# New pacing constants for a hand-planned two-layer transformer kernel

## The chip, the cores and the metric

The kernel runs on one core of a Trainium2 chip. The metric is the device time of one execution in microseconds. The engines are TensorE (PE, with its weight loads PEld), VectorE (DVE), ScalarE (ACT), GpSimd (POOL) and SyncE (SP), which here only issues transfers.

## What is computed

Two rounds of the same attention layer and the same feed-forward layer, with the same weights in both rounds, over 2048 tokens of 448 features in bfloat16. Attention has 16 heads of 28 features.

```python
x = A_x
x = x + _A_ref(_layernorm(x), A_wqkv, A_wo)
x = x + _B_ref(_layernorm(x), B_w1, B_b1, B_w2, B_b2)
x = x + _A_ref(_layernorm(x), A_wqkv, A_wo)
x = x + _B_ref(_layernorm(x), B_w1, B_b1, B_w2, B_b2)

# _A_ref: q, k, v of x @ wqkv; p = softmax(q k^T * 28 ** -0.5); (p v) @ wo
# _B_ref: h = relu(x @ w1 + b1); (h * h) @ w2 + b2
```

## The kernel before, in words

**Tiling.** A tile of scores, a unit, is 128 keys x 512: two key blocks of 128 by 256 queries of one head (four key blocks by 128 queries in the last two query blocks). There are 2048 units. They are taken in passes: a pass is one layer, one block of queries, one set g of four heads, and a range of key blocks. The second layer's first passes cover only the first ten key blocks, then the other six, so that they can begin while the first layer's last rows are still in work.

**Groups.** `s_stream` (L1015 on) takes three units at a time. It multiplies them on TensorE into three banks of one PSUM tile `sc` (L1074), and `e_stream` has ScalarE take the exponential of the whole tile in one activation (L1100). There are 683 groups. At each group `apart` may decide that the third unit goes aside: ScalarE then takes two banks, 1024 columns, and VectorE takes the third with GpSimd's help. That way is `a_unit` and `a_rest`: VectorE reads the scores once into integers (L1161), GpSimd or VectorE makes a mantissa line (L1190) and a power of two (L1204), VectorE squares (L1207), either adds one (L1210) or leaves that term to TensorE as a second multiplication with the values, and multiplies the two (L1213).

**Values and chains.** `p_stream` multiplies the exponentials with the values (L1297) and hands the sums on to be normalised. When a block's four sets of heads are done, `chain` does the output projection, the layernorm, the feed-forward layer, and for the first layer the next layernorm and the keys, values and queries of the second layer. All dense matmuls of the chains go through one helper (L782); K, Q and V are written to SBUF at L805, L801 and L833, the layernorm's transposes are at L685 and L697, and the residual sums at L1433.

**What sets the order.** A planner, `Planner.run`, simulates the engines in Python while the program is being written. Each stream offers its next operation; the one that can start earliest goes next, and ties go to the lower rank. Its result is a fixed order of instructions on each engine; nothing of it is decided on the chip. Constants steer it, and `s_stream` replaces some of them at certain groups:

```python
globals().update(PACE.get(gi, {}))
```

The ones that matter here, as `apart` and others use them:

- `FORCE` and `SKIP` are lists of group numbers. A group on the first always sends its third unit aside if buffers, data and position allow it; one on the second never does.
- Otherwise a unit goes aside only if VectorE's planned load over the last `SPAN` us is not above `BUSY` (or `LOW`), and its planned backlog in us not above `TB` (or `TB2`). `LOW` and `TB2` count when the layer's chains are behind a due line that `L1N` and `MARGIN` set. `LEAD` is the number of groups before VectorE's first unit. With fewer than `STOP` = 80 units left, none goes aside.

```python
if len(gbuf) - 1 in FORCE:
    return j
if len(gbuf) - 1 in SKIP or pl.load(SPAN, "DVE") > (LOW if behind(i) else BUSY):
    return None
if max(0.0, pl.clock["DVE"] - now) + left[0] > (TB2 if behind(i) else TB):
    return None
```

- `SPARE` and `VSPARE`: more free buffers than this, and the unit's "add one" becomes a second multiplication on TensorE in place of L1210 on VectorE.
- `MORE` limits how often a group's score matmuls are repeated into the same banks where TensorE would otherwise be idle (L1074 again; the result is the same).
- `C_PRIO`, `V_PRIO`, `V_LATE`, `V_LAST`, `V_AGE`, `V_PAST`, `V_WAIT`, `EPRIO`, `EV`: ranks of VectorE's and GpSimd's operations for the scores, and of the evacuations of the chains' matmuls. `PRE` moves a chain up before its rows are done.
- `KEEP`, `CHUNK`, `NEAR`, `FAR`, `LAG`: how long the multiplications with the values wait, how many of them go together, and how far ahead VectorE's unit is taken.
- `PWAIT`, `PNEAR`, `PORTP`: how VectorE and GpSimd take turns, in the plan, for operations marked as using a shared port.

Of the kernel before, what the change touches and what calls it, by code (L numbers as in the profile page):

```python
# [33 lines left out]
PWAIT = 3.0  # L34
PNEAR = 0.2
PORTP = 0.0
PGAP = 0.08
EPRIO = 6
SPARE = 1
VSPARE = 2  # L40
ASIDE = 2.0
# [6 lines left out]
PRE = 0.5  # L48
# [10 lines left out]
L1N = 5.6  # L59
MARGIN = 1.5  # L60
LOW = 0.85
# [12 lines left out]
SLACK = 0.5  # L74
WINDOW = 2.8
HTURNS = 3
C_PRIO = 1.6
V_PRIO = 8.5
V_LATE = 3.5
V_LAST = 2.5  # L80
V_AGE = 6
V_PAST = 2
# [3 lines left out]
V_WAIT = 5  # L86
NEAR = 3
FAR = 9
KEEP = 6
# [6 lines left out]
LAG = 12  # L96
LEAD = 15
LAST = 690
BUSY = 0.97
TB = 2.2  # L100
TB2 = 0.9
SPAN = 15
# [4 lines left out]
MORE = 1  # L107
# [6 lines left out]
SOON = 0.3  # L114
# [6 lines left out]
CHUNK = 2  # L121
EV = 2.9
# [13 lines left out]
MMC = 0.46  # L136
VGAP = 0.03
QP = 8
FORCE = (21, 50, 64, 78, 99, 101, 106, 137, 153, 155, 160, 179, 215, 218, 222, 233, 252, 300, 305, 324, 334, 363,
         373, 404, 443, 466, 487, 495, 533, 565, 568, 591, 593, 628, 633, 646)  # L140
SKIP = (0, 10, 29, 41, 43, 54, 57, 59, 62, 100, 105, 108, 110, 177, 195, 217, 219, 236, 293, 303, 335, 360, 378,
        383, 389, 395, 400, 408, 411, 418, 442, 467, 470, 471, 481, 494, 504, 544, 549, 558, 563, 571, 584, 588,
        601, 607, 613, 615, 630, 636)
PACE = {
    0: {'BUSY': 1.05, 'LOW': 1.0, 'CHUNK': 2, 'EV': 2.9, 'FAR': 9, 'KEEP': 2, 'L1N': 5.2, 'LAG': 8, 'LEAD': 10,
         'MARGIN': -1, 'MORE': 1, 'PRE': 0.5, 'SLACK': 0.7, 'SPAN': 11, 'TB': 2.0, 'TB2': 0.9, 'V_AGE': 6, 'V_LAST':
         3, 'V_PAST': 2, 'C_PRIO': 1.6, 'V_PRIO': 2.6, 'V_LATE': 6, 'V_WAIT': 5, 'EPRIO': 6, 'ASIDE': 2.0, 'SPARE':
         0, 'VSPARE': 2, 'NEAR': 3, 'SOON': 0.3, 'VGAP': 0.03, 'PWAIT': 3.0, 'PNEAR': 0.2, 'PORTP': 0.0},
    8: {'TB': 2.8, 'SPAN': 8},
    16: {'SPARE': 3, 'V_AGE': 3, 'C_PRIO': 1.2},  # L150
    24: {'PNEAR': 0.25, 'V_PRIO': 7, 'V_AGE': 2},
    32: {'BUSY': 0.95, 'V_PAST': 0},
    40: {'MORE': 3, 'BUSY': 1.06, 'SPARE': 1},
    48: {'MORE': 1},
    56: {'V_WAIT': 2, 'PWAIT': 1},
    64: {'VSPARE': 1, 'TB2': 2.0},
    72: {'EV': 3.5, 'MARGIN': 3},
    80: {'LAG': 3, 'SOON': 0.6, 'EV': 2.2},
    88: {'ASIDE': 0, 'LOW': 0.8, 'MORE': 3},
    96: {'SPAN': 11, 'LOW': 1.05, 'V_PAST': 5},  # L160
    104: {'V_PAST': 0},
    120: {'KEEP': 6},
    128: {'PRE': 0, 'LAG': 5},
    136: {'TB': 2.2},
    144: {'TB': 1.6, 'PWAIT': 0.3, 'SPAN': 6},
    152: {'CHUNK': 3, 'MORE': 1},
    160: {'SOON': 1.5, 'PRE': 1.2},
    168: {'V_PRIO': 6, 'VSPARE': 5, 'V_LATE': 3.5, 'VGAP': 0},
    184: {'NEAR': 6},
    192: {'ASIDE': 0.2, 'BUSY': 0.95, 'TB': 2.0},  # L170
    200: {'NEAR': 9},
    208: {'TB': 1.6, 'SPAN': 8, 'PWAIT': 1},
    216: {'LEAD': 15, 'BUSY': 1.02, 'EV': 1.3},
    224: {'FAR': 17, 'PORTP': 1, 'V_LATE': 2.6},
    232: {'LOW': 0.9, 'V_LAST': 2.2, 'PWAIT': 0.3, 'V_PRIO': 4, 'CHUNK': 2},
    248: {'V_LAST': 3.5, 'PRE': 0},
    256: {'C_PRIO': 2.1, 'V_PAST': 3},
    264: {'LAG': 12, 'SPARE': 0},
    272: {'VGAP': 0.15, 'SPARE': 3, 'EPRIO': 3},
    288: {'V_LATE': 4.6, 'VGAP': 0, 'EPRIO': 6, 'SPARE': 1, 'NEAR': 3},  # L180
    296: {'FAR': 9, 'PWAIT': 0.6, 'V_PRIO': 6, 'PNEAR': 0.35, 'TB2': 3.0, 'LOW': 0.8, 'NEAR': 6},
    304: {'PRE': 0.3},
    312: {'NEAR': 9, 'LOW': 0.9, 'LAG': 8, 'FAR': 6},
    320: {'MORE': 3, 'LOW': 1.05},
    328: {'CHUNK': 1, 'PORTP': 0.3, 'VSPARE': 2, 'V_PAST': 0},
    336: {'V_LAST': 2.2, 'V_AGE': 3},
    344: {'KEEP': 2, 'VGAP': 0.06, 'VSPARE': 20},
    352: {'PNEAR': 0.25},
    360: {'PRE': 0},
    368: {'TB': 2.4, 'PRE': 0.5, 'MORE': 1},  # L190
    376: {'C_PRIO': 1.2, 'MORE': 3, 'V_LATE': 2.6},
    392: {'PWAIT': 4, 'TB': 4.2},
    400: {'ASIDE': 0.5, 'TB': 3.4, 'NEAR': 3, 'V_LATE': 3.5, 'PORTP': 1, 'V_AGE': 6},
    408: {'EPRIO': 2.2, 'BUSY': 0.95, 'VSPARE': 2, 'LOW': 0.8},
    416: {'V_AGE': 3},
    424: {'V_LATE': 2.6, 'PWAIT': 0.6},
    432: {'V_LAST': 3.5},
    440: {'TB': 2.4, 'V_LAST': 2.2, 'LAG': 3, 'KEEP': 4},
    448: {'KEEP': 6, 'MARGIN': -6},
    456: {'SLACK': 0.5, 'V_LAST': 3.5, 'ASIDE': 1, 'PORTP': 0.3, 'C_PRIO': 1.6, 'MORE': 1, 'LEAD': 12},  # L200
    464: {'CHUNK': 3, 'LOW': 1.0, 'C_PRIO': 1.2},
    472: {'VGAP': 0.03, 'MORE': 3},
    480: {'NEAR': 9},
    488: {'CHUNK': 1, 'EPRIO': 4, 'V_PAST': 3},
    504: {'PWAIT': 1, 'LAG': 12},
    520: {'NEAR': 6, 'PRE': 0.3, 'C_PRIO': 1.6, 'V_LAST': 2.5, 'SPARE': 0},
    528: {'CHUNK': 2},
    536: {'SPARE': 3, 'EV': 2.2},
    560: {'PWAIT': 0.6, 'MORE': 1, 'MARGIN': -3, 'LEAD': 15},
    576: {'SLACK': 0.7, 'PNEAR': 0.35},  # L210
    584: {'MARGIN': 3},
    592: {'SPAN': 20, 'V_LAST': 3, 'NEAR': 9, 'SPARE': 1},
    600: {'PWAIT': 2, 'V_LAST': 2.5, 'LEAD': 18, 'KEEP': 2, 'PNEAR': 0.25},
    608: {'LOW': 0.9, 'EV': 2.9},
    632: {'V_PRIO': 7, 'MARGIN': 0.5},
    640: {'L1N': 5.8, 'KEEP': 4, 'V_AGE': 2},
}


# [177 lines left out]
def kernel(  # L397
# [536 lines left out]
    def behind(i):  # L934

        l = 0 if i < L0E else 1
        a, b, n = ((280, L0E, L0N), (1440, L1E, L1N))[l]
        return done[l] < (min(i, b) - a) / (b - a) * n * per[l] - MARGIN
# [16 lines left out]
    def apart(i, now, us, soon=SOON):  # L955
# [20 lines left out]
        if any(pl.tok.get(d) is None or pl.tok[d].end + LAT["DVE"] > now for d in needs(units[j])):  # L976
# [5 lines that stand above are left out]
# [620 lines left out]
```

## Time and profile before

| | |
|---|---|
| median of 3 runs | 825.06 us (825.05 to 825.16) |
| the profiled execution's own time | 826.26 us |
| its span, first to last instruction | 824.5 us |
| ScalarE busy | 804.9 us, 98% |
| TensorE matmuls busy | 791.2 us, 96% |
| VectorE busy | 768.6 us, 93% |
| GpSimd busy | 424.1 us, 51% |
| mean granted TensorE clock | 0.998 |

How to read it: "L1100 ACT" is the instruction that line 1100 issues on ScalarE. A row of a group gives its shapes, its number, the busy time and the mean duration of one in ns, and then the idle time of the engine just before such instructions with what ended it. A row of the waits gives the total in us, the number of times and the longest. A row of the timeline gives start, duration, engine and line, and in brackets the idle time before it. Durations of operations that follow each other on one engine overlap a little, so the busy time is less than number times mean.

### The profile page before, as it was taken

The page shows a single profiled execution, that of the slowest core. Times are in us where ns is not written, and L with a number is a line of the kernel's source. Part 1 is how long each engine was busy: PE and PEld are TensorE (multiplying, and loading weights), DVE is VectorE, ACT ScalarE, POOL GpSimd, SP SyncE. Part 2 cuts the span into 40 slices and gives each one's busy share as a digit, 9 for nine tenths or more (in the row PEclk, how much of TensorE's full clock was granted, in tenths as well). Part 3 has the DMA queues.
Part 4 walks back from the last instruction along what each step waited for, and adds up shares of the span by engine and source line. Part 5 has one row for each costly group of instructions (what it writes and reads, how often), then busy time and mean ns, then how long its engine had stood idle before and what let it go on. Part 6 is the DMA issues. An engine that isn't in the chain of part 4 may idle for free.

```text
span 824.5 us, 29048 instructions
## 1 busy us (share of the span) xinstructions
PE 791.2 (96%) x12174; PEld 426.4 (52%) x12174; DVE 768.6 (93%) x1801; ACT 804.9 (98%) x703; POOL 424.1 (51%) x683
## 2 busy tenths in 40 slices
PE   8999999999999999999999999889999999999997
PEld 4455554554555555545454554445454545445665
DVE  7999999999999999999999999999999999998553
ACT  8999999999999999999999998999999999999994
POOL 3356666555554554534445556663656666664100
PEclk9999999999999999999999999999999999999999
DMA  9200000000000000000000000011100000000000
GB/s 254 71 3 2 16 22 23 16 16 16 16 3 16 16 15 16 16 16 2 2 3 2 2 2 2 16 29 30 28 14 21 22 21 21 27 20 9 21 9 18
DMA packets 32319, 18.01 MB, mean 22 GB/s; under 512 B 17786, under 2 KB 31739, under 8 KB 32188
## 3 DMA queue, kind: packets, MB, share of 16 engines
q1 hardware_dynamic: 32188, 16.16, 7.0%
q8 instruction: 95, 1.56, 0.8%
q14 instruction: 36, 0.29, 0.1%
HBM read 13.87 MB, written 2.06 MB: 19 GB/s over the span
## 4 chain that ended last, share of the span: by engine, by line
PE 43%; ACT 32%; DVE 14%; issue 9%; POOL 1%; DMA 0%; SPq 0%; ACTq 0%; POOLq 0%; DVEq 0%
ACT pt L1100 31%; PE mt L782 17%; PE sc L1074 14%; PE oT L1297 10%; DVE pt L1213 2%; DVE r L1493 1%; DVE pt L1207 1%; DVE v_y L1161 1%; DVE K_sb L1161 1%; PE tp L685 1%; DVE st L632 1%; DVE x_sb L1433 1%; DVE V_sb L1161 1%; PE sc L782 1%; DVE xn L745 1%
## 5 line engine op out<-in xcount | busy, mean ns | idle before, releaser
L1100 ACT ACTIVATE pt<-sc 128x1536 bf16<-128x1536 f32 (+1 forms) x683 | 791.2, 1347 | 6.4 <-PE sc L1074 5.9
L1074 PE MATMUL sc<-Q_sb,K_sb 32*128 32x256 bf16 (+1 forms) x4820 | 286.2, 265 | 24.6 <-ACT pt L1100 18.5
L1074 PEld LDWEIGHTS <-K_sb 32*128 32x128 bf16 x4820 | 108.4, 92 | 197.4 <-issue 130.7
L1297 PE MATMUL oT<-pt,V_sb 128*32 128x256 bf16 (+1 forms) x4102 | 162.8, 269 | 1.0 <-DVE K_sb L697 0.3
L1297 PEld LDWEIGHTS <-V_sb 128*32 128x32 bf16 x4850 | 120.0, 96 | 56.4 <-issue 49.8
L782 PE MATMUL mt<-xnT,w 128*128 128x256 bf16 (+1 forms) x888 | 117.8, 271 | 0.1
L1161 DVE TENSOR_SCALAR v_y<-sc 128x512 int32<-128x512 f32 x160 | 108.4, 681 | 2.8 <-PE sc L1074 2.2
L782 PEld LDWEIGHTS <-w 128*128 128x128 bf16 x952 | 77.9, 98 | 34.1 <-issue 25.2
L1190 POOL TENSOR_SCALAR pt<-v_y 128x512 f16<-128x512 uint16 x94 | 60.9, 648 | 56.4 <-ACT pt L1100 9.6
L1204 POOL TENSOR_SCALAR v_y<-v_y 128x512 int16<-128x512 int16 x94 | 61.3, 652 | 40.3 <-DVE pt L1207 4.8
L1207 DVE TENSOR_TENSOR pt<-pt 128x512 f16<-128x512 f16 x184 | 75.1, 418 | 0.9 <-POOL pt L1190 0.9
L1493 DVE TENSOR_SCALAR r<-mt 128x512 bf16<-128x512 f32 x105 | 71.7, 683 | 3.8 <-PE mt L782 3.1
L782 PE MATMUL mt<-w,V_sb 128*128 128x448 bf16 (+2 forms) x288 | 68.3, 346 | 0.0
L1161 DVE TENSOR_SCALAR K_sb<-sc 128x512 int32<-128x512 f32 x80 | 54.1, 681 | 3.6 <-PE sc L1074 3.5
L1433 DVE TENSOR_TENSOR x_sb<-x_sb,mt 128x448 bf16<-128x448 bf16 (+2 forms) x62 | 37.3, 602 | 12.2 <-PE mt L782 12.1
L1204 POOL TENSOR_SCALAR K_sb<-K_sb 128x512 int16<-128x512 int16 x54 | 35.6, 658 | 22.5 <-DVE pt L1213 4.7
L1190 POOL TENSOR_SCALAR pt<-K_sb 128x512 f16<-128x512 uint16 x48 | 31.6, 658 | 29.6 <-DVE K_sb L1161 11.5
L1161 DVE TENSOR_SCALAR V_sb<-sc 128x512 int32<-128x512 f32 x62 | 42.1, 680 | 0.1
L632 DVE BATCH_NORM_STATS2 st<-x_sb 128x6 f32<-128x448 bf16 x62 | 37.9, 614 | 0.8 <-DMA x_sb<-in_A_x_dram 0.7
L782 PEld LDWEIGHTS <-V_sb 128*128 128x128 bf16 x302 | 24.6, 98 | 25.1 <-issue 11.8
L662 POOL TENSOR_TENSOR ve<-mv,eps_t 128x2 f32<-128x2 f32 (+1 forms) x33 | 8.1, 247 | 55.2 <-DVE mv L637 48.3
L1297 PE MATMUL oT<-K_sb,V_sb 128*32 128x256 bf16 (+1 forms) x254 | 35.8, 271 | 0.0
(158 smaller groups left out, 1112.9 us busy)
## 6 DMA issues: line engine op xcount, KB each, us to landing
rec<-scr SPq DMA_DIRECT2D x54, 128.0 KB
x_sb<-in_A_x_dram SPq DMA_DIRECT2D x8, 224.0 KB
out_dram<-x_sb SPq DMA_DIRECT2D x15, 112.0 KB
w<-in_B_w_dram SPq DMA_DIRECT2D x1, 1568.0 KB
w<-in_B_w_dram SPq DMA_DIRECT2D x1, 1344.0 KB
dn<-oT_sb SPq DMA_DIRECT2D x54, 4.0 KB
V_sb<-in_A_wqkv_dram SPq DMA_DIRECT2D x4, 168.0 KB
scr<-dn SPq DMA_DIRECT2D x27, 8.0 KB
```

Source lines behind the costliest of these rows:

```text
L632: nc.vector.bn_stats(out=box["st"][:, :], in_=x_sb[:, t0 + j, :] if src is None else src())
L782: nc.tensor.matmul(box["t"][:, c0:c0 + n], lhsT=lhsT() if callable(lhsT) else lhsT, rhs=rhs, start=a, stop=b)
L1074: nc.tensor.matmul(dst[k][:, i * nt * P:(i + 1) * nt * P], lhsT=K_sb[l][rows, g, (kb + i) * P:(kb + i + 1) * P], rhs=Q_sb[rows, g, t0 * P: ...
L1100: t = nc.scalar.activation(out=pt[:, 0:n], in_=gbuf[gi]["sc"][:, 0:n], func=AF.Exp, scale=float(np.log(2.0)) * 2.0 ** -FRAC)
L1161: t = nc.vector.tensor_scalar(out=y, in0=src, scalar1=EXP_BIAS, scalar2=EXP_LOW, op0=ALU.add, op1=ALU.max)
L1190: on(e).tensor_scalar(out=box["a"], in0=box["f"], scalar1=EXP_LINE[0], scalar2=EXP_LINE[1], op0=ALU.add, op1=ALU.mult)
L1204: on(e).tensor_scalar(out=box["e"].bitcast(DT.int16), in0=box["n"], scalar1=64.0, scalar2=EXP_BASE, op0=ALU.mult, op1=ALU.add)
L1207: nc.vector.tensor_tensor(out=box["a"], in0=box["a"], in1=box["a"], op=ALU.mult)
L1213: nc.vector.tensor_tensor(out=box["pd"], in0=box["aa"], in1=box["e"], op=ALU.mult)
L1297: nc.tensor.matmul(box["t"][DHP * hh:DHP * hh + DHP, 0:n], lhsT=V_sb[l][:, tb, 4 * g + hh, :], rhs=p, start=begin and j < G, stop=close an ...
L1433: nc.vector.tensor_tensor(out=x_sb[:, tb, lo:hi], in0=x_sb[:, tb, lo:hi], in1=t[:, 0:hi - lo], op=ALU.add)
L1493: nc.vector.tensor_scalar(out=r[:, 0:w], in0=t[:, 0:w], scalar1=0.0, scalar2=None, op0=ALU.max)
```

## The change

Only constants change: the list of groups that must send a unit aside (36 to 42), the list of those that must not (50 to 25), and the table of pacing constants, its first row (the values before the first group) and its later rows. The functions are the same, and so is the number of groups. What differs in the program is the order of instructions on each engine, which units VectorE and GpSimd take and how many, how many score matmuls are repeated, and how often the "add one" is done on VectorE.

```diff
-FORCE = (21, 50, 64, 78, 99, 101, 106, 137, 153, 155, 160, 179, 215, 218, 222, 233, 252, 300, 305, 324, 334, 363,
-         373, 404, 443, 466, 487, 495, 533, 565, 568, 591, 593, 628, 633, 646)
-SKIP = (0, 10, 29, 41, 43, 54, 57, 59, 62, 100, 105, 108, 110, 177, 195, 217, 219, 236, 293, 303, 335, 360, 378,
-        383, 389, 395, 400, 408, 411, 418, 442, 467, 470, 471, 481, 494, 504, 544, 549, 558, 563, 571, 584, 588,
-        601, 607, 613, 615, 630, 636)
+FORCE = (17, 47, 84, 107, 111, 144, 215, 237, 240, 241, 271, 322, 341, 347, 354, 363, 368, 379, 404, 413, 423, 428,
+         434, 438, 440, 453, 457, 472, 495, 512, 515, 532, 561, 608, 614, 628, 633, 640, 641, 648, 652, 667)
+SKIP = (20, 38, 46, 66, 190, 202, 227, 235, 246, 299, 302, 357, 362, 384, 461, 465, 474, 475, 489, 504, 520, 542,
+        607, 649, 650)
-    0: {'BUSY': 1.05, 'LOW': 1.0, 'CHUNK': 2, 'EV': 2.9, 'FAR': 9, 'KEEP': 2, 'L1N': 5.2, 'LAG': 8, 'LEAD': 10,
-         'MARGIN': -1, 'MORE': 1, 'PRE': 0.5, 'SLACK': 0.7, 'SPAN': 11, 'TB': 2.0, 'TB2': 0.9, 'V_AGE': 6, 'V_LAST':
-         3, 'V_PAST': 2, 'C_PRIO': 1.6, 'V_PRIO': 2.6, 'V_LATE': 6, 'V_WAIT': 5, 'EPRIO': 6, 'ASIDE': 2.0, 'SPARE':
-         0, 'VSPARE': 2, 'NEAR': 3, 'SOON': 0.3, 'VGAP': 0.03, 'PWAIT': 3.0, 'PNEAR': 0.2, 'PORTP': 0.0},
-    8: {'TB': 2.8, 'SPAN': 8},
-    16: {'SPARE': 3, 'V_AGE': 3, 'C_PRIO': 1.2},
-    24: {'PNEAR': 0.25, 'V_PRIO': 7, 'V_AGE': 2},
-    32: {'BUSY': 0.95, 'V_PAST': 0},
-    40: {'MORE': 3, 'BUSY': 1.06, 'SPARE': 1},
-    48: {'MORE': 1},
-    56: {'V_WAIT': 2, 'PWAIT': 1},
-    64: {'VSPARE': 1, 'TB2': 2.0},
-    72: {'EV': 3.5, 'MARGIN': 3},
-    80: {'LAG': 3, 'SOON': 0.6, 'EV': 2.2},
-    88: {'ASIDE': 0, 'LOW': 0.8, 'MORE': 3},
-    96: {'SPAN': 11, 'LOW': 1.05, 'V_PAST': 5},
-    104: {'V_PAST': 0},
-    120: {'KEEP': 6},
-    128: {'PRE': 0, 'LAG': 5},
-    136: {'TB': 2.2},
-    144: {'TB': 1.6, 'PWAIT': 0.3, 'SPAN': 6},
-    152: {'CHUNK': 3, 'MORE': 1},
-    160: {'SOON': 1.5, 'PRE': 1.2},
-    168: {'V_PRIO': 6, 'VSPARE': 5, 'V_LATE': 3.5, 'VGAP': 0},
-    184: {'NEAR': 6},
-    192: {'ASIDE': 0.2, 'BUSY': 0.95, 'TB': 2.0},
-    200: {'NEAR': 9},
-    208: {'TB': 1.6, 'SPAN': 8, 'PWAIT': 1},
-    216: {'LEAD': 15, 'BUSY': 1.02, 'EV': 1.3},
-    224: {'FAR': 17, 'PORTP': 1, 'V_LATE': 2.6},
-    232: {'LOW': 0.9, 'V_LAST': 2.2, 'PWAIT': 0.3, 'V_PRIO': 4, 'CHUNK': 2},
-    248: {'V_LAST': 3.5, 'PRE': 0},
-    256: {'C_PRIO': 2.1, 'V_PAST': 3},
-    264: {'LAG': 12, 'SPARE': 0},
-    272: {'VGAP': 0.15, 'SPARE': 3, 'EPRIO': 3},
-    288: {'V_LATE': 4.6, 'VGAP': 0, 'EPRIO': 6, 'SPARE': 1, 'NEAR': 3},
-    296: {'FAR': 9, 'PWAIT': 0.6, 'V_PRIO': 6, 'PNEAR': 0.35, 'TB2': 3.0, 'LOW': 0.8, 'NEAR': 6},
-    304: {'PRE': 0.3},
-    312: {'NEAR': 9, 'LOW': 0.9, 'LAG': 8, 'FAR': 6},
-    320: {'MORE': 3, 'LOW': 1.05},
-    328: {'CHUNK': 1, 'PORTP': 0.3, 'VSPARE': 2, 'V_PAST': 0},
-    336: {'V_LAST': 2.2, 'V_AGE': 3},
-    344: {'KEEP': 2, 'VGAP': 0.06, 'VSPARE': 20},
-    352: {'PNEAR': 0.25},
-    360: {'PRE': 0},
-    368: {'TB': 2.4, 'PRE': 0.5, 'MORE': 1},
-    376: {'C_PRIO': 1.2, 'MORE': 3, 'V_LATE': 2.6},
-    392: {'PWAIT': 4, 'TB': 4.2},
-    400: {'ASIDE': 0.5, 'TB': 3.4, 'NEAR': 3, 'V_LATE': 3.5, 'PORTP': 1, 'V_AGE': 6},
-    408: {'EPRIO': 2.2, 'BUSY': 0.95, 'VSPARE': 2, 'LOW': 0.8},
-    416: {'V_AGE': 3},
-    424: {'V_LATE': 2.6, 'PWAIT': 0.6},
-    432: {'V_LAST': 3.5},
-    440: {'TB': 2.4, 'V_LAST': 2.2, 'LAG': 3, 'KEEP': 4},
-    448: {'KEEP': 6, 'MARGIN': -6},
-    456: {'SLACK': 0.5, 'V_LAST': 3.5, 'ASIDE': 1, 'PORTP': 0.3, 'C_PRIO': 1.6, 'MORE': 1, 'LEAD': 12},
-    464: {'CHUNK': 3, 'LOW': 1.0, 'C_PRIO': 1.2},
-    472: {'VGAP': 0.03, 'MORE': 3},
-    480: {'NEAR': 9},
-    488: {'CHUNK': 1, 'EPRIO': 4, 'V_PAST': 3},
-    504: {'PWAIT': 1, 'LAG': 12},
-    520: {'NEAR': 6, 'PRE': 0.3, 'C_PRIO': 1.6, 'V_LAST': 2.5, 'SPARE': 0},
-    528: {'CHUNK': 2},
-    536: {'SPARE': 3, 'EV': 2.2},
-    560: {'PWAIT': 0.6, 'MORE': 1, 'MARGIN': -3, 'LEAD': 15},
-    576: {'SLACK': 0.7, 'PNEAR': 0.35},
-    584: {'MARGIN': 3},
-    592: {'SPAN': 20, 'V_LAST': 3, 'NEAR': 9, 'SPARE': 1},
-    600: {'PWAIT': 2, 'V_LAST': 2.5, 'LEAD': 18, 'KEEP': 2, 'PNEAR': 0.25},
-    608: {'LOW': 0.9, 'EV': 2.9},
-    632: {'V_PRIO': 7, 'MARGIN': 0.5},
-    640: {'L1N': 5.8, 'KEEP': 4, 'V_AGE': 2},
+    0: {'BUSY': 1.05, 'LOW': 1.0, 'CHUNK': 2, 'EV': 2.9, 'FAR': 6, 'KEEP': 2, 'L1N': 5.2, 'LAG': 3, 'LEAD': 18,
+         'MARGIN': -1, 'MORE': 1, 'PRE': 0.5, 'SLACK': 0.7, 'SPAN': 11, 'TB': 1.6, 'TB2': 0.9, 'V_AGE': 6, 'V_LAST':
+         3, 'V_PAST': 2, 'C_PRIO': 1.6, 'V_PRIO': 8.5, 'V_LATE': 3.5, 'V_WAIT': 5, 'EPRIO': 6, 'ASIDE': 2.0,
+         'SPARE': 1, 'VSPARE': 2, 'NEAR': 3, 'SOON': 0.3, 'VGAP': 0.03, 'PWAIT': 1, 'PNEAR': 0.2, 'PORTP': 0.0},
+    8: {'V_PAST': 5, 'LEAD': 12},
+    16: {'SPAN': 8, 'EPRIO': 4, 'SPARE': 3, 'PRE': 0.8},
+    24: {'V_AGE': 2},
+    32: {'V_AGE': 8},
+    40: {'MORE': 3, 'V_LAST': 2.5},
+    48: {'MORE': 1, 'TB2': 3.0},
+    56: {'VSPARE': 1},
+    64: {'TB': 2.0, 'PNEAR': 0.15, 'MARGIN': 1.5},
+    72: {'KEEP': 6},
+    88: {'PWAIT': 4, 'TB2': 0.6, 'C_PRIO': 1.2},
+    96: {'EV': 1.3},
+    104: {'EPRIO': 6, 'V_PAST': 0, 'CHUNK': 3},
+    120: {'V_LAST': 3, 'PWAIT': 1, 'SPARE': 1, 'L1N': 5.6},
+    128: {'TB': 4.2},
+    136: {'TB': 2.2, 'V_AGE': 3},
+    144: {'TB': 1.6, 'V_LAST': 2.2, 'V_LATE': 4.6, 'PWAIT': 4},
+    152: {'V_AGE': 5},
+    176: {'EV': 2.2},
+    184: {'V_LAST': 3, 'SPARE': 0},
+    240: {'SPAN': 15, 'LOW': 0.8},
+    248: {'V_PAST': 2, 'PORTP': 1},
+    272: {'SPARE': 3},
+    280: {'MARGIN': -3, 'SPARE': 1},
+    288: {'VGAP': 0, 'NEAR': 9},
+    296: {'SPARE': 0, 'SOON': 0.6},
+    312: {'V_AGE': 6},
+    320: {'PWAIT': 0.6},
+    328: {'V_LAST': 2.2},
+    336: {'V_AGE': 4, 'V_PAST': 3, 'L1N': 5.8},
+    344: {'VSPARE': 2},
+    360: {'V_PAST': 5},
+    368: {'PNEAR': 0.25},
+    376: {'V_LAST': 2.5, 'V_AGE': 3},
+    384: {'SPARE': 2},
+    392: {'SPARE': 1},
+    400: {'EPRIO': 4},
+    408: {'VSPARE': 1, 'NEAR': 6},
+    416: {'SOON': 1, 'TB': 2.0},
+    424: {'PORTP': 0},
+    440: {'V_LATE': 2.6, 'V_LAST': 3},
+    456: {'MARGIN': 0.5, 'LOW': 0.9, 'V_PRIO': 4},
+    464: {'PRE': 0.5},
+    496: {'L1N': 5.0},
+    512: {'VSPARE': 3, 'KEEP': 4, 'V_LAST': 2.2},
+    520: {'BUSY': 1.02, 'ASIDE': 0},
+    528: {'V_AGE': 5, 'V_WAIT': 2},
+    536: {'EV': 1.5, 'VSPARE': 1, 'SPAN': 8},
+    552: {'V_AGE': 2, 'C_PRIO': 1.6},
+    560: {'V_LAST': 3, 'PORTP': 1},
+    608: {'L1N': 5.6},
+    616: {'L1N': 5.8, 'LAG': 12, 'V_LATE': 3.5, 'SPARE': 2},
+    624: {'VSPARE': 20},
+    632: {'ASIDE': 0.5},
+    640: {'SPARE': 3},
+    648: {'V_LAST': 2.5},
+    664: {'CHUNK': 2, 'L1N': 5.0},
```

## The prediction

> **What bounds the kernel now.** I read the page's busy line and the activations by shape first, then ScalarE's waits, windows of busy time, and the timelines of ScalarE, VectorE and TensorE where those pointed.
>
> ```profile
> PE 791.2 (96%) x12174; PEld 426.4 (52%) x12174; DVE 768.6 (93%) x1801; ACT 804.9 (98%) x703; POOL 424.1 (51%) x683
> L1100 ACT ACTIVATE pt<-sc 128x1536 bf16<-128x1536 f32 x380 | 547.8, 1531 | 2.7 <-PE sc L1074 2.6
> L1100 ACT ACTIVATE pt<-sc 128x1024 bf16<-128x1024 f32 x303 | 316.2, 1116 | 3.7 <-PE sc L1074 3.3
> L1161 DVE TENSOR_SCALAR v_y<-sc 128x512 int32<-128x512 f32 x160 | 108.4, 681 | 2.8 <-PE sc L1074 2.2
> L1207 DVE TENSOR_TENSOR pt<-pt 128x512 f16<-128x512 f16 x184 | 75.1, 418 | 0.9 <-POOL pt L1190 0.9
> L1213 DVE TENSOR_TENSOR pt<-pt,v_y 128x512 bf16<-128x512 f16 x49 | 21.9, 446 | 0.3
> L1210 DVE TENSOR_SCALAR pt<-pt 128x512 f16<-128x512 f16 x38 | 12.2, 325 | 0.1
> ```
>
> ScalarE works 98% of the span, and nearly all of it is 683 exponentials: 380 over three banks, 303 over two. A two-bank group is one whose third bank of scores went to VectorE and GpSimd. So the end is set by how many groups are of two banks, and by where ScalarE waits. It waits for scores only, and in few places:
>
> ```profile
> ACT pt L1100 <- PE sc L1074: 5.9, 6, 3.1
> ...
> 511.91 0.68 DVE L805 CAST K_sb<-mt 128x512 bf16<-128x512 f32 x1
> 512.65 0.61 PE L1074 MATMUL sc<-Q_sb,K_sb 32*128 32x256 bf16 x11 [0.78 <-DVE K_sb L805]
> 513.14 13.70 ACT L1100 ACTIVATE pt<-sc 128x1024 bf16<-128x1024 f32 x12 [3.10 <-PE sc L1074]
> ...
> 40.00:760.00 720.00, 694.92 (x10503) 367.37 (x10500) 698.80 (x1613) 715.58 (x627) 404.40 (x640) 1.00 0.05 14
> 200.00:510.00 310.00, 303.13 (x4448) 158.99 (x4448) 300.63 (x707) 309.77 (x267) 157.68 (x262) 1.00 0.03 8
> 552.00:554.00 2.00, 1.76 (x18) 1.14 (x20) 1.60 (x4) 2.00 (x3) 1.21 (x2) 0.64 0.27 83
> 554.00:556.00 2.00, 2.00 (x27) 0.93 (x30) 1.98 (x5) 1.47 (x2) 0.70 (x2) 0.51 0.08 12
> 778.81 28.09 ACT L1100 ACTIVATE pt<-sc 128x1536 bf16<-128x1536 f32 x21
> ```
>
> The reader is to see four things. At 510 us ScalarE stands for 3.10 us: the second layer's scores need a K block whose cast ends at 512.6 (the seam of the layers). From 40 to 760 us VectorE is idle for only 21.2 us and TensorE for 25.1 (columns: PE, PEld, DVE, ACT, POOL, granted clock, DMA share, GB/s). At 552 to 556 the granted clock falls to half for some 3.4 us, and two ScalarE waits follow (0.18 and 0.68). And 21 three-bank exponentials in a row take 28.09, 1.338 each; the 791.2 us in exponentials then leave (791.2 - 380 x 1.338) / 303 = 0.933 for a two-bank one. One more two-bank group is thus worth 0.40 us of ScalarE; the median from start to start (1.330 and 0.904) gives 0.43. I take 0.42.
>
> **The frame.** The profiled execution took 826.26: 1.8 outside the span, 9.5 to the first exponential, 797.4 to the end of the last, 17.6 after. The median of the runs is 1.2 lower (825.06); the sum's difference is carried over to it.
>
> **The change, part by part.** No instruction's form changes; constants decide group by group which work goes where and when.
>
> 1. *Which groups have two banks.* I counted the activations in order and laid the lists on them. Of the 42 groups newly forced, 667 is past the point where VectorE's share ends (group 656); 28 are two-bank already, so at most +13. Of the 25 newly barred, 10 are two-bank now: -10. Of the old 50 barred groups 48 are released (504 and 607 stay): 0 to +48. Of the old forced, 26 that are two-bank lose it as a must: 0 to -26. Positions alone thus bound it at -36 to +51, too wide to use. VectorE bounds it: a bank costs it 0.681 + 0.418 + 0.446 = 1.55, with the addition at L1210 (60 times in 302, 0.325) 1.61. Its 21.2 idle us hold 13 more: -5.5 us at most. Below, the backlog limits are tighter (TB 1.6, then 2.0 from group 416, where it was 2.4 to 4.2 from 368; TB2 0.6 from 88, where it was up to 3.0): I take eight groups fewer, +3.4 us, as the other end (a sixth of 48). GpSimd's two passes (1.30 a bank) lie in its 315 idle us. Between the ends I take +6: -2.5 us.
>
> 2. *The addition, VectorE's or TensorE's.* All 60 additions at L1210 lie between 232 and 530 us, where VSPARE was 5, 2 and 20 in turn; it becomes 1 to 2 there. If three quarters of them go (an estimate), VectorE gains 45 x 0.325 = 14.6 us (room for 9 banks, which is why I stand at +6 and not at 0), and TensorE gets two more 256-column matmuls each time, at 0.11 from start to start 0.22: 9.9 us. Its idle time from 200 to 510 is 6.9, but repeated score passes fill more. I cost it at nothing; without that cover it costs 9.9 - 6.9 = 3.0.
>
> 3. *The seam.* The 3.10 us wait is the end of a chain of a normalisation, transpose, projection and cast, 507.6 to 513.1; it goes if the first layer's chains start that much earlier. Ranks of chains (C_PRIO, EV, PRE) and L1N all change. Fewer VectorE additions and fewer repeats favour an earlier chain; the nine forced groups between 404 and 457 speak against it. Ends: gone (-3.1) and doubled (+3.1). I take half gone: -1.5. Late next would be the following K cast.
>
> 4. *Fewer repeated score passes.* MORE falls to 1 in groups 88 to 152, 320 to 368, 376 to 456 and 472 to 560, where it was 3. The repeats fill gaps of TensorE, for example
>
> ```profile
> 115.22 0.83 PE L1074 MATMUL sc<-Q_sb,K_sb 32*128 32x256 bf16 x18 [0.52 <-ACT pt L1100]
> ```
>
> where 18 matmuls stand for six. Taken by itself that frees nothing on the path. But the one stretch at half clock (552.5 to 555.9) comes in groups 456 to 472, where MORE already was 1. In the 3.41 us before it matmul columns streamed for 40% of the time (starts from the trace, 0.107 us per 256 columns); stretches at 47% kept the clock. I took the third and fourth passes out of the trace in those groups: three to five stretches then fall under 43%, near 113, 126, 530 and 537 us. One such drop costs 0.18 + 0.68 = 0.86. Ends: none left (-0.9), five instead of one (+3.4). The new plan will fill these stretches otherwise, so I take one more: +0.9. The Trainium skill (TensorE: Matmul & The Clock Gate, Part 1) says that the clock halves after at least one idle window of about 3.4 us; the drop above, with columns streaming for 40%, does not agree. By the page's rule this term would be 0 and the time 0.9 lower.
>
> 5. *Rest.* Turns at the shared VectorE and GpSimd port (PWAIT, PNEAR, PORTP): the final multiply at L1213 totals 10.8 us above its median of 0.416 over 302 runs; a tenth either way, 1 us of VectorE, is 0.3 on the end. Opening: LEAD 18 falls to 12 at group 8, and VectorE's first bank is at group 11 now; 0, bounds 0.4 either way (one bank). After the last exponential 17.6 us remain with the same work: 0, at most 0.5. Transfers stay out of it: the mean DMA share is 0.05 and no wait of ScalarE ends on one.
>
> Sum: -2.5 + 0 - 1.5 + 0.9 + 0 = -3.1: 823.2 on the profiled execution, 822.0 on the median.
>
> **The rivals.**
> *Deeper gain.* Thirteen more two-bank groups and the seam gone with the clock as now: -5.5 - 3.1 = -8.6 at most; half to all of it gives 816.5 to 820.8. For: VectorE's 21 idle us. Against: it never came nearer to full than 97%. I put it at 819, chance 0.12.
> *The clock* (the other side). Four more half-clock stretches at 0.86 and the other gains absent: 828.5. It decides from four stretches on (3.4 against the 4.0 of terms 1 and 3 leaves nothing measurable). For: the 40% and 47% above, and that MORE has no part in the order except to fill gaps. Against: TensorE is 97% busy over 40 to 760, and other work can fill the gaps. Chance 0.16.
> *TensorE short of time.* The 60 additions moved onto it all lie where it is 98% busy: +3.0, 828.1; from 6.9 us of additions (31) on. Against: it waited 18.5 us for ScalarE in the score passes, so some slack is there. Chance 0.10.
> *Tighter backlog, fewer banks for VectorE:* +3.4, 828.5. For: TB and TB2. Against: half as many barred groups. Chance 0.08.
> *Nothing measurable:* the released groups are used but others fall, and the seam stays: 825.1, chance 0.14.
>
> **How the numbers follow.** The forecast (820.8 to 823.4) has 0.40, the deeper gain 0.12 and the three slower rivals 0.34. I call 0.2% (1.65 us) the bound of what can be told from no change: faster 0.52, same 0.14, slower 0.34. The range reaches over the deeper gain's middle to the slower rivals' sums and a little beyond: 818.5 to 829.
>
> **What would show it.** Step 1: the two-bank row at x309 instead of x303, and L1161 up by as many. Step 2: L1210 at some 15 instead of 60, more matmuls at L1297. Step 3: ScalarE's longest wait under 2 us near 510. Step 4: the granted clock under 1.00 in two stretches, beyond the end. I am wrong if the two-bank row falls, if ScalarE's total wait on L1074 passes 10 us, or if the exponentials take longer each without waiting.

## The result and the profile after

The changed kernel takes 819.39 us (median of 6 runs, 817.41 to 821.79), the old one beside it 825.2 us. The ratio is 0.9924, 95% interval 0.9905 to 0.9943: 0.8% faster. The prediction was 822.0, range 818.5 to 829.

The table of constants is 13 lines shorter, so every line number of the code below it is 13 lower: L1100 is now L1087, L1161 is L1148, L1210 is L1197. First the page's busy line, the groups of instructions by shape, and ScalarE's waits, of the changed kernel:

```profile
PE 783.8 (96%) x12133; PEld 427.8 (52%) x12133; DVE 768.5 (94%) x1784; ACT 801.3 (98%) x700; POOL 422.9 (52%) x678
L1087 ACT ACTIVATE pt<-sc 128x1536 bf16<-128x1536 f32 x377 | 546.1, 1528 | 2.5 <-PE sc L1061 2.1
L1087 ACT ACTIVATE pt<-sc 128x1024 bf16<-128x1024 f32 x306 | 321.9, 1102 | 1.4 <-PE sc L1061 1.3
L1148 DVE TENSOR_SCALAR v_y<-sc 128x512 int32<-128x512 f32 x163 | 110.5, 680 | 2.4 <-PE sc L1061 1.8
L1197 DVE TENSOR_SCALAR pt<-pt 128x512 f16<-128x512 f16 x10 | 3.3, 331 | 0.0
...
ACT pt L1087 <- PE sc L1061: 3.4, 6, 1.1
```

There are 306 two-bank groups, three more than before. ScalarE's waits for scores fell from 5.9 to 3.4 us. The additions on VectorE fell from 60 to 20 (10 of them in the row shown, the rest in rows of other tile names). Then the timelines around the layers' seam, and windows of busy time, of the changed kernel:

```profile
496.74 0.69 DVE L792 CAST K_sb<-mt 128x512 bf16<-128x512 f32 x1 [0.29 <-PE mt L769]
494.18 26.70 ACT L1087 ACTIVATE pt<-sc 128x1024 bf16<-128x1024 f32 x24
...
40.00:760.00 720.00, 693.95 (x10554) 372.68 (x10554) 697.08 (x1590) 717.70 (x629) 399.18 (x630) 1.00 0.05 14
200.00:510.00 310.00, 303.46 (x4513) 162.24 (x4508) 298.24 (x670) 309.93 (x271) 177.44 (x288) 1.00 0.03 9
532.00:536.00 4.00, 3.48 (x53) 1.84 (x49) 3.40 (x9) 4.00 (x4) 2.85 (x5) 0.73 0.07 10
552.00:556.00 4.00, 4.00 (x55) 2.27 (x54) 3.19 (x7) 2.97 (x4) 2.06 (x4) 0.71 0.18 54
803.27:817.40 14.13, 11.10 (x140) 8.38 (x137) 6.61 (x18) 3.71 (x8) 0.56 (x1) 0.99 0.06 17
```

The K block that the seam waits for (the first layer's last block of rows, its first two sets of heads) is cast at 496.7 us, where the old kernel had it at 511.9, and 24 exponentials follow each other across the seam without a wait. In two places, not one, the granted clock falls to half. VectorE is as full as it was. And only 14.13 us are left after the last exponential. The same stretch of the old kernel, to compare:

```profile
806.90:824.50 17.60, 13.12 (x174) 10.21 (x172) 6.96 (x19) 5.77 (x10) 0.56 (x1) 1.00 0.05 15
```

In the two profiled executions the span fell from 824.5 to 817.4, by 7.1. I call waits what the exponentials took from start to start beyond their medians (1.330 us for three banks, 0.904 for two); a wait counts at the group that starts before it.

| part of the span, us | before | after | difference |
|---|---|---|---|
| to the first exponential | 9.47 | 9.57 | +0.1 |
| exponentials at their medians: three more two-bank groups | | | -1.3 |
| waits at groups 384 to 447 (the seam) | 4.2 | 0.9 | -3.3 |
| waits at groups 448 to 511 (where the clock halves) | 1.6 | 3.5 | +1.8 |
| waits elsewhere | 12.1 | 11.1 | -1.1 |
| last exponential itself, past its median | | | +0.1 |
| after the last exponential | 17.6 | 14.1 | -3.4 |

Not all of the +1.8 is the clock. Experiments 3 and 6 ran the changed order without a half-clock stretch there and still have 1.7 us of waits at groups 448 to 511, so two stretches account for 1.7 of the 3.5; by this estimate one more stretch is 0.9 of the +1.8, and what the rest waits for stays open.

How often the clock halves differs from run to run of one kernel, so the runs can be sorted by it (number of stretches = (1 - mean clock) x 2 x span / 3.41; the old kernel's runs are those taken beside the experiments):

| half-clock stretches | old kernel: runs, mean span | changed kernel: runs, mean span |
|---|---|---|
| 0 | 17, 823.4 | 1, 815.4 |
| 1 | 9, 824.5 | 3, 817.0 |
| 2 | 8, 825.6 | 2, 817.8 |

In the old kernel each costs 1.1 us. The changed kernel's six runs, 1.6 for the first and 0.7 for the second, fit that but are too few to say more. The old one has 0.74 in the mean, the changed one 1.17. At an equal number the change is worth 7.5 to 8.0 us; a mean 0.5 of that is given back through the clock. The medians differ by less, 5.8, because an old run of 825.2 has no stretch and the changed runs around 819.39 have one. The profiled execution of the changed kernel took 821.79, of which 4.4 lie outside the span, against 1.8 to 2.2 in its other five runs; the reason is not recorded. The Trainium skill (TensorE: Matmul & The Clock Gate, Part 1) states that the activity window runs freely and does not start with the kernel; runs of one fixed order with none, one and two stretches agree with that.

### The profile page after: what moved, and what is told of

The parts are those of the page before. It is cut to its first block, busy times and chain, and to the rows that moved or that the text cites. A ratio compares the mean times of both kernels' runs of the same rounds, so it can differ in the third digit from the quotient of the medians.

```text
span 817.4 us, 28983 instructions
## 1 busy us (share of the span) xinstructions
PE 783.8 (96%) x12133; PEld 427.8 (52%) x12133; DVE 768.5 (94%) x1784; ACT 801.3 (98%) x700; POOL 422.9 (52%) x678
## 4 chain that ended last, share of the span: by engine, by line
PE 69%; ACT 16%; DVE 10%; issue 3%; DMA 1%; POOL 0%; ACTq 0%; SPq 0%; DVEq 0%
PE mt L769 29%; PE sc L1061 22%; PE oT L1284 16%; ACT pt L1087 16%; PE tp L672 2%; DVE v_y L1148 1%; DVE r L1480 1%; DVE st L619 1%; DVE pt L1200 1%; PE sc L769 1%; DVE K_sb L1148 1%; DVE K_sb L792 1%; DMA rec<-scr 1%; DVE pt L1194 1%; DVE xn L732 0%
## 5 line engine op out<-in xcount | busy, mean ns | idle before, releaser
L1087 ACT ACTIVATE pt<-sc 128x1536 bf16<-128x1536 f32 (+1 forms) x683 | 789.8, 1337 | 3.9 <-PE sc L1061 3.4
L1284 PEld LDWEIGHTS <-V_sb 128*32 128x32 bf16 x4922 | 127.9, 96 | 47.4 <-issue 40.6
L1284 PE MATMUL oT<-pt,V_sb 128*32 128x256 bf16 (+1 forms) x4196 | 151.6, 269 | 0.0
L1177 POOL TENSOR_SCALAR pt<-v_y 128x512 f16<-128x512 uint16 x121 | 78.5, 648 | 98.9 <-DVE v_y L1148 29.7
L1148 DVE TENSOR_SCALAR v_y<-sc 128x512 int32<-128x512 f32 x163 | 110.5, 680 | 2.4 <-PE sc L1061 1.8
L1194 DVE TENSOR_TENSOR pt<-pt 128x512 f16<-128x512 f16 x234 | 96.4, 423 | 3.4 <-POOL pt L1177 3.3
L769 PE MATMUL mt<-w,V_sb 128*128 128x448 bf16 (+1 forms) x288 | 68.9, 348 | 0.0
L1191 POOL TENSOR_SCALAR v_y<-v_y 128x512 int16<-128x512 int16 x70 | 45.5, 650 | 30.6 <-DVE pt L1194 9.3
L1148 DVE TENSOR_SCALAR K_sb<-sc 128x512 int32<-128x512 f32 x81 | 55.0, 680 | 1.6 <-PE sc L1061 1.4
L1420 DVE TENSOR_TENSOR x_sb<-x_sb,mt 128x448 bf16<-128x448 bf16 (+1 forms) x62 | 37.5, 604 | 9.4 <-PE mt L769 9.0
L1177 POOL TENSOR_SCALAR pt<-V_sb 128x512 f16<-128x512 uint16 x45 | 30.2, 671 | 24.3 <-DVE V_sb L1148 7.8
L1148 DVE TENSOR_SCALAR V_sb<-sc 128x512 int32<-128x512 f32 x61 | 41.5, 680 | 1.2 <-PE sc L1061 0.9
L1200 DVE TENSOR_TENSOR pt<-pt,K_sb 128x512 bf16<-128x512 f16 x92 | 39.8, 433 | 0.3
L1284 PE MATMUL oT<-K_sb,V_sb 128*32 128x256 bf16 x214 | 34.1, 274 | 0.0
```

What stands on the lines that cost most here:

```text
L769: nc.tensor.matmul(box["t"][:, c0:c0 + n], lhsT=lhsT() if callable(lhsT) else lhsT, rhs=rhs, start=a, stop=b)
L1087: t = nc.scalar.activation(out=pt[:, 0:n], in_=gbuf[gi]["sc"][:, 0:n], func=AF.Exp, scale=float(np.log(2.0)) * 2.0 ** -FRAC)
L1148: t = nc.vector.tensor_scalar(out=y, in0=src, scalar1=EXP_BIAS, scalar2=EXP_LOW, op0=ALU.add, op1=ALU.max)
L1177: on(e).tensor_scalar(out=box["a"], in0=box["f"], scalar1=EXP_LINE[0], scalar2=EXP_LINE[1], op0=ALU.add, op1=ALU.mult)
L1191: on(e).tensor_scalar(out=box["e"].bitcast(DT.int16), in0=box["n"], scalar1=64.0, scalar2=EXP_BASE, op0=ALU.mult, op1=ALU.add)
L1194: nc.vector.tensor_tensor(out=box["a"], in0=box["a"], in1=box["a"], op=ALU.mult)
```

## The experiments

Experiments 1, 2, 9, 10 and 12 join the two kernels at a group: the lists and the table of one up to it, those of the other from there. The first row of the second part then holds all of that kernel's values in force at that group, so only what lies before differs.

**1. New constants to group 575, old from there.**

```diff
 PACE = {
 ...
     560: {'V_LAST': 3, 'PORTP': 1},
-    608: {'L1N': 5.6},
-    616: {'L1N': 5.8, 'LAG': 12, 'V_LATE': 3.5, 'SPARE': 2},
-    624: {'VSPARE': 20},
 ...
+    576: {'BUSY': 0.95, 'LOW': 1.0, 'CHUNK': 2, 'EV': 2.2, 'TB': 2.4, 'TB2': 3.0, ...},
+    584: {'MARGIN': 3},
 ...
```

> The changed kernel's constants up to group 575, the old ones from there. Group 576 starts at 673.7 us in the changed kernel's trace, and the old constants took 128.8 us from there to the last exponential. Theory A (the shorter end is bought: between groups 576 and 640 VectorE takes fewer banks, 25 for 30, and the last chains get ahead): 30 or more two-bank groups there, the last exponential ends before 803.3, and the end after it is back at 17.6 us or more, so the span is 820 or more, against 817.4. Rival B (the shorter end comes from what lies before group 576): the end stays near 14.1 us and the span at 817 or less.

825.97 us, ratio 1.0001 (0.9988 to 1.0014): all of the gain in time is gone. (These runs have more half-clock stretches than the old kernel's; at an equal number their spans are still 1.1 to 1.7 us shorter.) The activations by shape, ScalarE's longest wait and the timeline's end, and the window after the last exponential:

```profile
L1082 ACT ACTIVATE pt<-sc 128x1024 bf16<-128x1024 f32 x311 | 324.3, 1096 | 1.4 <-PE sc L1056 1.3
ACT r L1473 <- PE sc L764: 9.3, 2, 9.0
...
794.76 6.45 ACT L1082 ACTIVATE pt<-sc 128x1536 bf16<-128x1536 f32 x5
810.20 0.60 ACT L1473 ACTIVATE r<-sc 128x512 bf16<-128x512 f32 x1 [8.98 <-PE sc L764]
...
803.00:824.10 21.10, 17.37 (x187) 12.53 (x186) 7.87 (x19) 5.07 (x9) 0.56 (x1) 1.00 0.07 23
```

Theory A holds, and strongly. With 311 two-bank groups the exponentials end at 801.2, 2.1 us before those of the changed kernel, and the span is 824.1 against 817.4: 22.8 us are left after the last exponential. TensorE has 17.4 us of work from 803.0 on, where the changed kernel has 11.1 from 803.3 on. VectorE took 32 banks between 576 and 640, against 25. In groups 608 to 639 alone it took 17 against 9, and there the chains' dense matmuls kept TensorE busy for 12.6 us against 19.7; what was not done there was left for the end, where these matmuls take 18.7 us against 10.7. That the banks are what held the chains back is argued from this: with them, all other constants from group 576 on were exchanged too.

**2. The halves exchanged: old to group 575, new from there.**

```diff
 PACE = {
 ...
     560: {'PWAIT': 0.6, 'MORE': 1, 'MARGIN': -3, 'LEAD': 15},
-    576: {'SLACK': 0.7, 'PNEAR': 0.35},
-    584: {'MARGIN': 3},
 ...
+    576: {'BUSY': 1.02, 'LOW': 0.9, 'CHUNK': 3, 'EV': 1.5, 'TB': 2.0, 'TB2': 0.6, ...},
+    608: {'L1N': 5.6},
 ...
```

> The old constants up to group 575, the new ones from there. Group 576 starts at 678.1 us in the old kernel's trace, and the new constants took 129.6 us from there to the last exponential. Theory A: the end after the last exponential falls to about 14 us, the span to about 821.8. Rival B: it stays near 17.6, the span near 825. Rival C (the constants of the end work only on the state that they were found for): fewer two-bank groups and no shorter end, 825 or more.

826.76 us, ratio 1.0013 (1.0000 to 1.0026). The last exponential ends at 809.9 and the span at 824.9, so 15.0 us are left, 2.6 less than in the old kernel; but 299 two-bank groups and new waits (0.9 us at group 581, 0.7 at 634) put the exponentials 3.0 later. Theory A is right on the end, C on the sum: these constants do shorten the end on the state that the other kernel left too, and lose as much ahead of it.

**3. Repeats wherever the plan has a gap, in the same order.** The plan's own times are left as they were, so every instruction other than the added matmuls stands where it stood.

```diff
-                for i in list(range(4)) * (again + 1):
+                wide = again
+                if short > 0 and 1 <= gi < 683:
+                    wide = max(again, min(3, int(min(o.room, last - LAT["PE"] - 0.05 - o.end) / 0.22)))
+                for i in list(range(4)) * (wide + 1):
```

> The changed kernel with its order of work kept as it is; only where a gap of TensorE has room for it by the plan, a group's score matmuls are issued up to three times more instead of once more. Theory (half-clock stretches cost about 1 us each; the changed kernel's waits at groups 456, 469 and 470 are theirs, 2.3 us together): the granted clock stays at 1.000, the waits at these groups go, and the time is 817 to 818.5 in every run, 1 to 2 us under the changed kernel's median of 819.4. Rival (the clock costs nothing there, and more passes delay TensorE): 819.5 to 822.

820.81 us, ratio 0.9946 (0.9928 to 0.9965). The clock did stay whole in three of four runs, and the waits for the clock went: from group 448 to 512 the exponentials took 74.1 us instead of 75.8. But with 228 matmuls added (4712 to 4940) group 448 begins 2.3 us later: there are 24 small waits of 0.2 to 0.5 us in the whole stream instead of 8. At whole clock the span is 818.9, and 815.4 in the changed kernel's one run of that kind. The time is the rival's, and of the reasons each holds a half: a half-clock stretch costs over a microsecond, and repeats in gaps that the plan takes for free are not free.

**4. No repeats from group 88 to 559, in the same order.**

```diff
-                for i in list(range(4)) * (again + 1):
+                for i in list(range(4)) * (1 if 88 <= gi < 560 else again + 1):
```

> The changed kernel with its order kept; from group 88 to 559 no score matmul is repeated. Theory (the repeats keep the clock): four or more half-clock stretches instead of two in the profile, 2 to 4 us slower than the changed kernel, 821.5 to 823.5. Rival (a half-clock stretch costs nothing where TensorE has gaps): within 0.7 us of the changed kernel.

820.17 us (819.38 to 822.01), ratio 0.9937 (0.9918 to 0.9956). Without 216 matmuls the profiled execution still has only two half-clock stretches, at 534 and 544 us; the four runs have 2, 2, 3 and 5 (spans 817.5, 817.7, 818.9, 820.1), where further ones lie in the longer runs is not recorded. So the repeats do keep some of the clock, three stretches a run without them against 1.2 with them, but less than I expected, and the time lies between the two forecasts: in the profiled execution the early places that the prediction named, near 113 and 126 us, stay whole.

**5. Repeats at groups 446 to 473 alone.**

```diff
-                if short > 0 and 1 <= gi < 683:
+                if short > 0 and 446 <= gi < 474:
```

> The changed kernel with its order kept; score matmuls are issued up to three times more, where the plan leaves a gap, in groups 446 to 473 alone (526 to 556 us). With that done everywhere, the stretch from group 448 to 512 fell from 75.8 to 74.0 us, and the stretches before it grew by 2.3. Theory (a half-clock stretch costs 1.1 us, and passes elsewhere only delay): clock 1.000 in most runs, span about 815.5 to 816.3, time 817.4 to 818.3 and a spread under 1.5 us. Rival (the added passes cost as much here as they save): 819 to 820, like the changed kernel.

819.33 us (819.10 to 820.00), ratio 0.9919 (0.9905 to 0.9934): the changed kernel's time. In the profiled execution the stretch at 534 is gone and one at 550 is left; by the mean clocks the other three runs have one, one and two, where is not recorded. The plan's gaps there had room for 30 more matmuls, and that was not enough to keep the clock. The rival's number came out, though not for its reason: at one stretch the spans are 817.1 to 817.6, against 816.2 to 817.6 without the added passes.

**6. Second multiplications left out, groups 150 to 429.**

```diff
-                            if j < len(v):
+                            if j < len(v) and not 150 <= v[j][2] < 430:
```

> The changed kernel with its order kept; in groups 150 to 429 the second multiplication with the values (in place of the addition on VectorE) is left out, so that part of the result lacks a term. 121 units have it there (65 in the old kernel): 121 x 0.22 = 26.6 us of TensorE go. Theory (TensorE's second multiplications lie in its gaps): the last exponential ends within 1 us of the changed kernel's. Rival (TensorE short of time): it ends 2 us or more earlier, the small waits of ScalarE before group 430 shrinking.

819.40 us, ratio 0.9913 (0.9895 to 0.9932). TensorE in the window from 160 to 526 us, first the changed kernel and then this one:

```profile
160.00:526.00 366.00, 356.30 (x5320) 189.54 (x5322) 352.91 (x794) 365.90 (x322) 212.92 (x344) 1.00 0.04 9
```

```profile
160.00:526.00 366.00, 345.95 (x5092) 180.78 (x5090) 353.68 (x795) 365.97 (x322) 213.96 (x344) 1.00 0.04 9
```

228 matmuls in this window (242 in all) and 10.4 us of TensorE's busy time are gone, less than the 26.6 expected, and ScalarE's does not move. From group 128 to 448 the exponentials take 365.4 us, against 365.8. The last exponential ends 2.2 us earlier, which by the letter is the rival's sign; but 1.7 of it arise at groups 448 to 511, behind the edit, where this execution has no half-clock stretch and the changed kernel's has two. At an equal number the spans agree (815.2 and 815.4 without one). So the theory holds: in this order a TensorE that reads 97% busy hides them.

**7. The old kernel with short additions.**

```diff
-            nc.vector.tensor_scalar(out=box["a"], in0=box["a"], scalar1=1.0, scalar2=None, op0=ALU.add)
+            nc.vector.tensor_scalar(out=box["a"][:, 0:8], in0=box["a"][:, 0:8], scalar1=1.0, scalar2=None, op0=ALU.add)
```

> The old kernel with its order kept; the 60 additions at L1210 work on 8 columns instead of 512, so that part of the result lacks a term. Some 60 x 0.2 = 12 us of VectorE go, all between 232 and 530 us. Theory (time taken off VectorE is worth nothing by itself; it counts only where the plan makes more two-bank groups of it or earlier chains): within 1 us of the old kernel, the wait at 510 us still 2.5 us or more. Rival (VectorE's delay of the chains makes the wait at 510): the wait falls under 1.5 us and the span by as much.

825.15 us, ratio 0.9995 (0.9985 to 1.0005). ScalarE's waits for scores:

```profile
ACT pt L1094 <- PE sc L1068: 5.1, 4, 3.0
```

The additions' busy time fell by 7.4 us (19.5 to 12.1), less than the 12 expected, and the span by nothing; the wait at the seam stands at 3.0. The theory holds: in this fixed order, time taken off VectorE buys nothing.

**8. The new table with the old lists.**

```diff
-FORCE = (17, 47, 84, 107, 111, 144, 215, ...
+FORCE = (21, 50, 64, 78, 99, 101, 106, ...
-SKIP = (20, 38, 46, 66, 190, 202, 227, ...
+SKIP = (0, 10, 29, 41, 43, 54, 57, ...
```

> The new table of constants with the old lists of forced and barred groups. Theory (constants and lists fit each other only): slower than both kernels, above 830, with VectorE's banks at other groups and new waits of ScalarE for scores. Rival (the table carries the gain, the lists are details): 819 to 822.

851.70 us in one run, with 310 two-bank groups, more than either kernel has. ScalarE's waits:

```profile
ACT pt L1082 <- PE sc L1056: 18.2, 12, 10.8
ACT pt L1082 <- issue: 11.5, 2, 9.9
```

ScalarE stands for 9.9 us at group 345, where the second layer's scores begin, and for 10.8 at group 429, where the seam is. The theory holds; for 11.5 us of the waits the profile names no releaser, so their cause stays open. This run has something to say on the end, too: VectorE takes only 24 banks between groups 576 and 640, and yet 17.6 us are left after the last exponential, as in the old kernel. So few banks there do not make a short end by themselves.

**9. New constants to group 383, old from there.**

```diff
 PACE = {
 ...
     376: {'V_LAST': 2.5, 'V_AGE': 3},
-    384: {'SPARE': 2},
-    392: {'SPARE': 1},
 ...
+    384: {'BUSY': 1.02, 'LOW': 1.05, 'CHUNK': 1, 'EV': 1.3, 'TB': 2.4, 'TB2': 3.0, 'VSPARE': 20, ...},
+    392: {'PWAIT': 4, 'TB': 4.2},
 ...
```

> The new constants up to group 383, the old ones from there. In the changed kernel the first layer's last K block is cast at 496.7 us, in the old one at 511.9, where ScalarE waits 3.1 us for it. Theory (the chains get ahead before group 384, by what TensorE and VectorE do there): the cast comes before 505, and no wait over 1.5 us stands between groups 425 and 435. Rival (the constants from 384 on do it): cast after 508 and the wait at 3 us or more. The rest, if the old constants fitted this state, would be 454.5 + 350.5 - 3.1 = 801.9 for the last exponential; if they do not, there are new waits of ScalarE after group 435 and an end of over 17.6 us.

835.41 us in one run. VectorE's cast of that K block, and ScalarE behind it:

```profile
512.11 0.69 DVE L790 CAST K_sb<-mt 128x512 bf16<-128x512 f32 x1
...
513.35 6.88 ACT L1085 ACTIVATE pt<-sc 128x1024 bf16<-128x1024 f32 x6 [3.32 <-PE sc L1059]
```

My theory falls and the rival's signs are met: the seam is as late as in the old kernel.

**10. Old constants to group 383, new from there.**

```diff
 PACE = {
 ...
     376: {'C_PRIO': 1.2, 'MORE': 3, 'V_LATE': 2.6},
-    392: {'PWAIT': 4, 'TB': 4.2},
 ...
+    384: {'BUSY': 1.05, 'LOW': 0.8, 'CHUNK': 3, 'EV': 2.2, 'TB': 1.6, 'TB2': 0.6, 'VSPARE': 2, ...},
+    392: {'SPARE': 1},
 ...
```

> The old constants up to group 383, the new ones from there. Theory of the run with the halves exchanged: the cast of the first layer's last K block stays at 511 us or later, and ScalarE waits 3 us or more there. Rival: the wait goes. In both cases, if constants fit only the state that they were found in, the span is above 824.5, the old kernel's.

834.03 us in one run; the cast comes at 513.9 and ScalarE waits 6.7 us behind it:

```profile
515.24 1.94 ACT L1092 ACTIVATE pt<-sc 128x1024 bf16<-128x1024 f32 x2 [6.73 <-PE sc L1066]
```

The theory holds, and with experiment 9 neither half brings the chain forward by itself.

**11. The new lists with the old table.**

```diff
-PACE = {0: {..., 'FAR': 6, 'LAG': 3, 'LEAD': 18, 'TB': 1.6, ...}, 8: {'V_PAST': 5, 'LEAD': 12}, ...
+PACE = {0: {..., 'FAR': 9, 'LAG': 8, 'LEAD': 10, 'TB': 2.0, ...}, 8: {'TB': 2.8, 'SPAN': 8}, ...
```

> The new lists of forced and barred groups with the old table of constants. Theory (lists and table fit each other only; the other half of this pair came out at 849.9 with two waits of 10 us at the layers' seam): above 835, with ScalarE's waits for scores above 10 us in total and a two-bank count that is not lower than 300. Rival (the lists carry the gain): 819 to 822.

864.34 us in one run, with 308 two-bank groups:

```profile
ACT pt L1094 <- PE sc L1068: 31.5, 19, 14.1
```

The longest of these, 14.1, is at the seam again (group 430). The theory holds here too: neither the lists nor the table carries any of the gain alone.

**12. New constants to group 431, old from there.**

```diff
 PACE = {
 ...
     424: {'PORTP': 0},
-    440: {'V_LATE': 2.6, 'V_LAST': 3},
 ...
+    432: {'BUSY': 0.95, 'LOW': 0.8, 'CHUNK': 1, 'EV': 1.3, 'TB': 3.4, 'TB2': 3.0, 'V_LAST': 3.5, ...},
+    440: {'TB': 2.4, 'V_LAST': 2.2, 'LAG': 3, 'KEEP': 4},
 ...
```

> The new constants up to group 431, the old ones from there. With the change made at 384 the first layer's last K block was cast at 512.1 us in this order and at 513.9 in the other, so neither half alone brings it forward. Theory (the constants of groups 384 to 431 bring the chain forward, on the state that the new ones left): cast at about 497, no wait over 1.5 us between groups 425 and 435. Rival (what comes after group 431 is needed as well): cast at 508 or later and the wait at 2.5 us or more.

834.13 us in one run. The cast and ScalarE's waits:

```profile
497.07 0.69 DVE L790 CAST K_sb<-mt 128x512 bf16<-128x512 f32 x1 [0.29 <-PE mt L767]
...
ACT r L1476 <- PE sc L767: 9.2, 2, 8.9
ACT pt L1085 <- PE sc L1059: 6.5, 11, 1.5
ACT pt L1085 <- PE oT L1282: 3.3, 2, 2.1
```

The theory holds for the seam: with the new constants and lists for groups 384 to 431 on the state that the new ones left, the cast is at 497.1 and no wait stands there. It does not hold for the time: later waits and 22.6 us after the last exponential make a span of 832.4. Which single constant among those of groups 384 to 431 does it was not tried and stays open.

## Why the prediction was right, point by point

The sign and the range were right; the forecast of -3.1 us was half of the -5.8 measured, and it was put together from some right terms and one that failed. The time lies in the band of the rival called deeper gain (816.5 to 820.8), not in the forecast's own (820.8 to 823.4), but it did not come that rival's way: there are three more two-bank groups, not thirteen, the clock is worse, and of its terms only the seam came true. That the range held is in part luck, since one term was 1.2 too large and two were too small.

*Which groups have two banks* (+6, -2.5): the mechanism was right and the size too big, +3 and -1.3. VectorE is no fuller than it was (697.1 us from 40 to 760, against 698.8). Experiments 1, 8 and 11 say more: 308 to 311 two-bank groups came with spans of 824 to 863 us. The count is not what decides; I had taken it for the main term.

*The additions* (at no cost): right. 40 of 60 went, and experiment 6 shows that in this order TensorE hides the second multiplications that took their place. That also settles the rival of TensorE short of time. That time taken off VectorE makes room for more banks was argued, and experiment 7 shows only that without a new plan it makes none.

*The seam* (half gone, -1.5): right in sign, too small. The wait went whole, with 3.3 us of delay at groups 384 to 447. The chain that it ends came 15 us earlier, not the 3 that would have been enough. I gave weight to the nine forced groups between 404 and 457; experiments 9, 10 and 12 show that the constants and lists of groups 384 to 431, on the state that the new ones leave before, bring the chain forward.

*The clock* (+0.9): right in sign and, by chance, near in size. A stretch costs 1.1 us in the old kernel, where I had 0.86 from the two waits alone, and there are 0.4 more of them a run, not one: +0.5. The rival that was built on it failed: four stretches came in none of the changed kernel's runs. Taking out third and fourth passes from the old order said little about a new order; the profiled execution of experiment 4 keeps the clock in the early places with no repeats at all. The 43% that I used as a limit does not hold either (last section).

*Rest* ("After the last exponential 17.6 us remain with the same work: 0, at most 0.5"): this is the step that failed, and its -3.4 us are the largest term of all. What remains after the last exponential isn't fixed: it is the part of the last chains that was not done beside the exponentials, and TensorE has 11.1 us of it instead of 13.1. Experiment 1 shows the trade: against the old constants from group 576 on, the new ones cost ScalarE 2.1 us and save 8.7 at the end. Fewer banks for VectorE go with it (25 against 32), and with experiment 2 (25 banks, 15.0 us left), but experiment 8 (24 banks, 17.6 us left) shows that their number alone does not decide. I had read the tighter backlogs (TB 2.0, TB2 0.6) as a loss of banks and nothing else; whether they or other constants of these groups make the trade was not tried one by one and stays open. The sentence on transfers was not quite right: in the old kernel one wait of ScalarE, 0.5 us at the opening, ends on one, and 0.8 in the changed kernel; the first exponential moves by 0.1.

## What to carry to other kernels

Where one engine is full to the end, the end still has two parts: when its stream stops, and what the other engines are left with then; a plan that gives the full engine a little more work late can be faster by several times that (in experiment 1, 2.1 us against 8.7). Constants that steer such a plan are right only together: the table alone and the lists alone lost about four and a half and nearly seven times what the whole set gains (26 and 39 us against 5.8), so compare whole plans, not their entries. And a wait at a seam is looked for where its chain starts, tens of microseconds ahead.

## What the runs showed of the hardware

The same order of instructions ran with zero to two half-clock stretches of 3.41 us (in other orders up to five), each worth 1.1 us in the old kernel, so single runs of one kernel lie apart by over 2 us while its order is fixed. Extra matmuls that keep the clock whole cost 3.5 us at whole clock when put into every gap of the plan (818.9 against 815.4, the latter one run), more than the stretches that they prevent (1.17 a run without them, 0.25 with them, at 1.1 us). And 10.4 us of TensorE's busy time could be taken out of a stretch in which it reads 97% busy without moving its end by more than 0.5 us. No single share of streaming time tells when the clock halves: by the prediction's count over the 3.41 us before, the stretches of the changed kernel follow 42% and 45%, those of experiments 2 and 9 follow 50%, and in both of these runs the clock stayed whole after a window at 45%.
